# Loads by SyncE and casts by GpSimd for pairs 4 to 7, a preferred score bank, the last row tile in columns, and a new order of units, in an attention and MLP-mixer kernel

## The chip, the cores and the metric

The kernel runs on one core of a Trainium2 chip. Times are device microseconds of one execution; "before" is the median of three runs. A profile is one more execution, taken by the hardware profiler. Engines are named as the profile names them: PE (TensorE matmul) and PEld (its weight load), DVE (VectorE), ACT (ScalarE), POOL (GpSimd), SP (SyncE). A trailing q (SPq, POOLq) means the engine's sequencer, which issues DMAs.

## The reference

Attention over 4 batches of 8 heads, 768 positions and 64 features, with a window of 128 keys and 4 sink keys, then an MLP mixer on the result (512 features in all): token mixing through 256 hidden tokens and channel mixing through 1536 hidden channels.

```python
scores = scale * np.matmul(q, k.transpose(0, 1, 3, 2))
keep = is_sink | in_window              # pos < 4, or 0 <= query - key < 128
scores = np.where(keep, scores, -1000000000.0)
a = softmax(scores)
x = np.matmul(a, v)                     # heads side by side: (4, 768, 512)
...
h = np.maximum(xt @ w_tok1, 0.0) @ w_tok2
u = x + h.transpose(0, 2, 1)
h2 = np.maximum(u @ w_ch1, 0.0) @ w_ch2
return u + h2
```

## The kernel before

**The work and its units.** Two heads of one batch make a pair; there are 16 pairs (p), four to a batch. For each pair q and k are loaded in rows, made bf16, and turned so that features lie on partitions (qT, kT). Scores are taken in three groups (g = 0, 1, 2) of two key tiles each, masked, put through exp, and multiplied with v, which carries a column of ones for the sums. The mixer works on a batch: hidden tokens (tile h1T), u, u turned (tile uT), hidden channels (tile v1T), and the output rows, six tiles of 128.

**The order of TensorE** is written out by hand in ORDERED (L47 to L56), as numbered units of named streams:

- s, m, t, o: the first four pairs (batch 0): scores, masks added by matmul, q or k turned (12 matmuls of L530), values. o5 and o6 are pair 2's two halves of values, s12 is pair 3's last score group.
- g, h: batch 0's token mixing for the first and second half of the features. g2 to g4 and h2 to h4 make u; g5 to g7 and h5 to h7 turn it (four matmuls each, L146).
- a: pairs 4 to 15. a0 and a1 turn pair 4's q and k; a2 turns pair 5's q and k (24 matmuls, L548) and takes pair 4's first scores; a4 and a8 do so for the pairs after. From pair 8 on (BY_DMA, L61) q and k are turned by DMA transposes on SP (L476) instead.
- k: token mixing of the later batches. c: 24 units a batch of hidden channels (4 matmuls with w_ch1). x: 24 units a batch of output (3 matmuls of 512 columns with w_ch2, four units to a row tile).

Everything else (which engine evicts, when a DMA is issued, which PSUM bank is taken) is settled when the program is written, by a planner (class Plan, L275): it holds costs in ns for each operation, a model of the DMA queue with eight transfers under way at most (LANES, L251), and at each step commits the operation that can begin first. Its times are not measured; they only fix each engine's order. Each engine then runs its own list strictly in order.

**PSUM.** Two score tiles of two banks each (sc0, sc1; L80) and four further banks. `Plan.choose` (L300) takes for a score group the score tile that was free first; a late unit may take a bank of sc1. Groups g = 1 and 2 of pairs 4 and up are written in quarters (matmuls on 64 keys, four side by side) when they fall on sc0 and in halves (128 keys) otherwise (by_halves and by_quarters, L586 to L611).

**Loads.** Pairs 0 to 3: q and k come as fp32 through SP (load_raw, L111; eight transfers of 384 KB) and are cast by ACT, DVE or POOL (cast, L1218). Pairs 4 to 15: POOL issues DMAs that cast to bf16 on the way (load_cast, L125; two for each q and each k, 96 KB each as landed). v (L133) and the weights (w_tok1, w_tok2, four quarters of w_ch1, four of w_ch2) are casting DMAs of POOL too. A POOL DMA waits until the one issued eight before it has landed. The order in which POOL's loads are queued is written at L1222 to L1245: v of pairs 1 to 3 with the token weights between, then pair 4 and the first two w_ch1 quarters, pair 5 and the other two, pairs 6 and 7, w_ch2, and the remaining pairs.

**The end.** `whole` (L1139) computes an output row tile: 12 matmuls of 512 columns into one bank, an addition of u on DVE (L1152), a store by SP (L1158).

All matmuls go through `mm` and stand at L143 in the profile; copies and casts stand at L150 (ACT) and L152 (DVE, POOL).

Of the kernel before, what the change touches and what calls it, by code (L numbers as in the profile page):

```python
# [16 lines left out]
def kernel(  # L17
# [29 lines left out]
    ORDERED = (  # L47
# [8 lines left out]
    )  # L56
# [194 lines left out]
    LANES = 8  # L251
    TURN, STORE = 1300.0, 700.0
    CROWDED = 2.4
# [5 lines left out]
    class Op:  # L259
        def __init__(self, cost, fn, deps=(), then=(), size=0.0, lag=None, loads=0, traffic=0.0):  # L260
            self.cost, self.fn, self.deps, self.then = cost, fn, list(deps), list(then)
            self.done = None
            self.lag = SEM if lag is None else lag
            self.size = size
            self.urgent = 0
            self.loads, self.traffic = loads, traffic
            self.need = {}
            self.half = False

    def landed(at):  # L270
# [4 lines left out]
    class Plan:  # L275
# [128 lines left out]
    def burst(*pieces):  # L404
# [6 lines left out]
        def run():  # L411
# [5 lines left out]
            [t for p in pieces for t in p.then], half=True,  # L417
        )
        for p in pieces:
            for key in p.keys:  # L420
                done[key] = op
# [157 lines left out]
    def scores(p, g):  # L579
# [70 lines left out]
        deps += [done["mask", p, g]] if by_pe else []  # L650
        return piece((190, 165, 140)[g] if quarters else width(g) * 0.47, run, deps, {} if by_pe else {"sc": [[x]]}, then, [("s", p)])

# [149 lines left out]
    def mix_h(b, g, t0, n):  # L802
# [26 lines left out]
        done.setdefault(("h", b, g), []).append(op)  # L829
        return unit(n * NT * cn * 0.422, run, of_group(b, g) + [done["tok1"]], {"mx": [[op]]}, [op])  # L830


    def mix_u(b, g, s0, n, by_pe=False):
# [26 lines left out]
        if pairs[BY_DMA][0] <= b:  # L860
# [7 lines left out]
            for half in range(s0 // QH, (s0 + n - 1) // QH + 1):  # L868
                done.setdefault(("uT", b, half), []).append(then[-1])
        return unit(n * (NTOK + by_pe) * cn * 0.422, run, done["h", b, g] + [done["tok2"]], {"mx": [[op]]}, then)  # L870

# [109 lines left out]
    def mix_channels(b):  # L981
        units = []

        def v1(ft, half):
# [18 lines left out]
            done["v1", b, ft, half] = op  # L1003
            return unit(648, run, done["uT", b, half] + [done["ch1", ft * NW // NF]], {"mx": [[op]]}, [op])

# [52 lines left out]
        def products(t0, n):  # L1058
# [42 lines left out]
            def product(m, bank_name, op, before, stored=()):  # L1101
                a_name, b_name = TERMS[m]
                units = []
                for c in range(2):
# [20 lines left out]
                    if before is not None:  # L1125
                        deps.append(before)
                    units.append(unit(
                        n * KC * 110, run, deps, {"mx": [banks[bank_name]]} if before is None and c == 0 else {},
                        [op, *stored] if c else [],
# [9 lines left out]
        def whole(st):  # L1139
# [24 lines left out]
            for f0 in range(0, NF, KC):  # L1164
                deps = [done["v1", b, ft, h] for ft in range(f0, f0 + KC) for h in range(2)]
                deps.append(done["ch2", f0 // KC])
                parts.append(unit(
                    KC * 216, lambda f0=f0: run(f0), deps, {"mx": [[o]]} if f0 == 0 else {},
                    [o, sent] if f0 == NF - KC else [],
                ))  # L1170
            return parts

        for c in range(2):
# [27 lines left out]
    plan = Plan()  # L1201
    plan.free.update(PE=3000.0, ACT=2200.0, DVE=3900.0, POOL=4100.0)
    plan.queue = 12200.0
# [13 lines left out]

    def cast(p, n, at):  # L1218
        cost = {"POOL": 850.0} if p == NHP - 1 else {"DVE": 570.0} if p or n else {"ACT": 850.0}
        return Op(cost, lambda e: copy(e, bf_tile(p, n), raws[p][n]), [landed(at)])  # L1220

    for p, at in enumerate(((3900.0, 5300.0), (7500.0, 8600.0), (11300.0, 12500.0), (13500.0, 14700.0))):  # L1222
        for n, name in enumerate(("q_bf", "k_bf")):
            queue((name, p), cast(p, n, at[n]))
    v_sink = Op({"POOL": 650.0}, lambda e: copy(e, v_sink0, v_sink_f), [landed(9000.0)])
# [106 lines left out]
```

## Time and profile before

| what | value |
|---|---|
| median of three runs | 207.27 us (206.79 to 207.35) |
| profiled execution: its time, its span | 206.17 us, 204.4 us |
| granted TensorE clock | 0.997 |
| busy: PE, DVE, ACT, POOL | 194.3, 103.0, 104.7, 75.2 us |
| instructions: PE, DVE, ACT, POOL | 1925, 228, 182, 110 |
| moved by DMA | 26.27 MB, 92261 packets, 82512 of them under 512 B |

The span runs from the first to the last instruction; the execution's own time has some 1.8 us around it. Rows of a timeline give start, length, engine, line, operation, output<-input, shape and count, and in brackets the idle time of the engine just before and what ended it. "Idle" is told from modelled ends of matmuls, so short gaps inside a run of matmuls don't show as idle. The DMA share is the mean of the busy shares of 16 DMA engines; it goes over 1 because several transfers of one engine overlap.

### The profile page before, as it was taken

Reading aid. Unit: us, or ns where it says so; the run is one execution under the profiler, and the core shown is the slowest. Engines: PE = TensorE matmul, PEld = TensorE weight load, DVE = VectorE, ACT = ScalarE, POOL = GpSimd, SP = SyncE. Lnnn points to the kernel's source line nnn. Section 1 sums busy time; section 2 is a strip of 40 time slices with the busy share of each in tenths; the row PEclk is TensorE's granted clock in tenths of the full one; section 3 lists DMA queues with packets and bytes.
Section 4 is the critical chain, followed back from the end, with each engine's and each line's share of the span. In section 5 each row is a group of like instructions: output and inputs, shape, how many; then the busy total and the mean of one; then the engine's idle time right before and its main releaser. Section 6 shows DMA issues by size and latency. Waiting matters only on the chain.

```text
span 204.4 us, 4672 instructions
## 1 busy us (share of the span) xinstructions
PE 194.3 (95%) x1925; PEld 114.0 (56%) x1945; DVE 103.0 (50%) x228; ACT 104.7 (51%) x182; POOL 75.2 (37%) x110
## 2 busy tenths in 40 slices
PE   6889898999999999999999999999999999999992
PEld 1356585666665654656655654666665455565440
DVE  4877656685676655533477675625532433001221
ACT  4967767877866115777772442567632003673000
POOL 6299958795695564664612040000000000000000
PEclk9999999999999999999999999999999999999998
DMA  5999999999999999999995663201021622100222
GB/s 201 290 254 186 171 177 190 157 175 200 159 136 126 156 162 240 138 155 212 156 113 108 181 125 111 79 2 26 3 49 54 106 103 83 47 0 3 103 103 103
DMA packets 92261, 26.27 MB, mean 129 GB/s; under 512 B 82512, under 2 KB 89168, under 8 KB 92240
## 3 DMA queue, kind: packets, MB, share of 16 engines
q0 software_dynamic: 67232, 11.80, 74.1%
q1 hardware_dynamic: 25008, 14.17, 31.2%
q8 instruction: 15, 0.25, 0.5%
q14 instruction: 6, 0.05, 0.1%
HBM read 26.75 MB, written 6.29 MB: 162 GB/s over the span
## 4 chain that ended last, share of the span: by engine, by line
PE 85%; DMA 5%; POOL 4%; DVE 2%; issue 1%; ACT 1%; SPq 0%; POOLq 0%
PE ps_mx L143 74%; PE ps_sc L143 9%; DMA q_bf<-in_q_dram 3%; DMA v_sink_f<-in_v_dram 2%; POOL v_aug L136 2%; POOL w_tok L161 1%; DVE kT L152 1%; PE ps_mx L518 0%; PE ps_mx L548 0%; PE ps_mx L146 0%; SPq L222 0%; POOL k_bf L152 0%; POOL q_bf L152 0%; POOL q_bf L128 0%; DVE o_sb L1152 0%
## 5 line engine op out<-in xcount | busy, mean ns | idle before, releaser
L143 PE MATMUL ps_mx<-w_ch,v1T 128*128 128x512 bf16 x271 | 65.1, 379 | 1.1 <-issue 0.3
L143 PE MATMUL ps_mx<-uT,w_ch 128*128 128x384 bf16 x352 | 62.7, 326 | 0.6 <-DVE uT L152 0.6
L619 ACT ACTIVATE pT<-ps_sc 128x1024 bf16<-128x1024 f32 (+1 forms) x48 | 44.0, 952 | 26.5 <-PE ps_sc L143 26.3
L156 ACT ACTIVATE v1T<-ps_mx 128x384 bf16<-128x384 f32 x74 | 36.2, 492 | 36.3 <-PE ps_mx L143 36.0
L143 PEld LDWEIGHTS <-w_ch 128*128 128x128 bf16 x384 | 36.2, 98 | 24.3 <-issue 2.0
L143 PEld LDWEIGHTS <-v1T 128*128 128x128 bf16 x288 | 27.1, 98 | 28.9 <-issue 0.6
L1152 DVE TENSOR_TENSOR o_sb<-ps_mx,u_sb 128x512 f32<-128x512 f32 x24 | 16.6, 690 | 37.2 <-PE ps_mx L143 35.2
L128 POOL DMA_DIRECT2D k_bf<-in_k_dram x24 | 19.7, 828 | 11.1 <-DMA v_aug<-in_v_dram 7.7
L128 POOL DMA_DIRECT2D q_bf<-in_q_dram x24 | 19.8, 835 | 8.4 <-DMA k_bf<-in_k_dram 4.2
L143 PEld LDWEIGHTS <-w_tok 128*128 128x128 bf16 x192 | 18.4, 98 | 6.2 <-issue 0.9
L850 DVE TENSOR_TENSOR u_sb<-ps_mx,x_sb 128x512 bf16<-128x512 f32 x19 | 12.9, 687 | 16.0 <-PE ps_mx L143 16.0
L136 POOL DMA_DIRECT2D v_aug<-in_v_dram x16 | 16.8, 1053 | 3.0 <-PE ps_mx L143 2.8
L143 PE MATMUL ps_sc<-qT,kT 64*128 64x256 bf16 (+2 forms) x240 | 16.7, 258 | 0.3
L143 PEld LDWEIGHTS <-pT 128*128 128x128 bf16 x352 | 14.2, 98 | 3.7 <-DVE x_sb L704 0.7
L637 DVE TENSOR_TENSOR pT<-pT,mask_main 128x1024 bf16<-128x1024 bf16 (+1 forms) x24 | 14.2, 618 | 2.4 <-ACT pT L619 2.4
L143 PE MATMUL ps_mx<-v_aug,pT 128*128 128x65 bf16 x297 | 13.7, 194 | 0.9 <-DMA v_aug<-in_v_dram 0.9
L158 DVE TENSOR_SCALAR v1T<-ps_mx 128x384 bf16<-128x384 f32 x14 | 7.8, 556 | 12.4 <-PE ps_mx L143 12.2
L143 PE MATMUL ps_mx<-h1T,w_tok 128*128 128x256 bf16 x92 | 13.7, 272 | 0.0
L143 PEld LDWEIGHTS <-kT 64*128 64x128 bf16 (+1 forms) x240 | 6.1, 98 | 10.9 <-issue 8.8
L143 PE MATMUL ps_mx<-x_sb,w_tok 128*128 128x256 bf16 x96 | 12.0, 273 | 0.0
L744 DVE TENSOR_TENSOR x_sb<-ps_mx,recip 128x384 bf16<-128x384 f32 x17 | 9.4, 554 | 0.3
L152 POOL COPY kTs<-kT 64x4 bf16<-64x4 bf16 x10 | 3.2, 321 | 16.0 <-DMA kT<-k_bf 15.6
(76 smaller groups left out, 148.5 us busy)
## 6 DMA issues: line engine op xcount, KB each, us to landing
out_dram<-o_sb SPq DMA_DIRECT2D x24, 256.0 KB, 2.2
v_aug<-in_v_dram POOLq DMA_DIRECT2D x16, 192.0 KB, 8.5
w_ch<-in_moe_w_ch_dram POOLq DMA_DIRECT2D x8, 384.0 KB, 8.9
q_bf<-in_q_dram POOLq DMA_DIRECT2D x24, 96.0 KB, 9.3
k_bf<-in_k_dram POOLq DMA_DIRECT2D x24, 96.0 KB, 8.2
q_f<-in_q_dram SPq DMA_DIRECT2D x4, 384.0 KB, 5.4
k_f<-in_k_dram SPq DMA_DIRECT2D x4, 384.0 KB, 6.0
w_tok<-in_moe_w_tok_dram POOLq DMA_DIRECT2D x2, 384.0 KB, 7.1
```

The costliest lines, as they stand in the source:

```text
L128: in_order(nc.gpsimd.dma_start(out=out[:, h], in_=rows[:, h]))
L136: in_order(nc.gpsimd.dma_start(out=v_aug.rearrange("p i t d -> p (i t) d")[:, :, 0:D], in_=v[b].rearrange("h s d -> (h s) d")[2 * hp * S:2 ...
L143: in_order(nc.tensor.matmul(*args, skip_group_check=True, **kwargs))
L152: in_order({"DVE": nc.vector, "POOL": nc.gpsimd}[e].tensor_copy(out=out, in_=in_))
L156: in_order(nc.scalar.activation(out, in_, AF.Relu))
L158: in_order(nc.vector.tensor_scalar_max(out=out, in0=in_, scalar1=0.0))
L161: return in_order(nc.gpsimd.dma_start(out=out, in_=in_))
L619: in_order(nc.scalar.activation(part(tiles["pT", p][:, :, ds(2 * g, 2)]), of_keys(tiles["ps_s", p, g])[:, :, 0:width(g)], AF.Exp, scale=scale,
L637: in_order(nc.vector.tensor_tensor(out=pt, in0=pt, in1=m, op=ALU.mult))
L744: in_order(nc.vector.tensor_tensor(out=x_sb[b][:, :, ds((2 * hp + i) * D, D)], in0=tiles["ps_o", p, i][:, :, 0:D], in1=tiles["recip", p, i ...
L850: in_order(nc.vector.tensor_tensor(out=u_part(b, g, s0, n), in0=tiles["ps_u", b, g, s0], in1=x_sb[b][:, s0:s0 + n, c0:c0 + cn], op=ALU.add,))
L1152: in_order(nc.vector.tensor_tensor(out=o_sb.rearrange("p (g c) -> p g c", g=2), in1=u_rows(b, st), in0=tiles["ps_out", b, st].rearrange("p ...
```

## The change

1. q and k of pairs 4 to 7 are loaded by SP as fp32 into the two buffers that pair 3's q and k came in, and cast by POOL. Each load waits for the cast that empties its buffer: pair 4's k goes into the buffer of pair 3's q, pair 4's q into that of pair 3's k, and so on crosswise, so that at most two are under way. POOL's casting DMAs for these pairs go; only v stays there. Pair 8 and later are as before.
2. For pairs 0 to 3, the casts may go to DVE or POOL (the first to ACT). In the program that comes out, pair 1's q is cast by POOL instead of DVE and pair 3's q by DVE instead of POOL.
3. Of the score tiles that are free by the time TensorE gets there, the first is taken; the planner's costs tell groups on sc0 and sc1 apart.
4. The last row tile of the last batch is computed in three pieces of columns (256, 128, 128), each with its own bank, addition and store.
5. ORDERED is another order, and some of the planner's costs and landing times are other numbers. Units o5, s12 and o6, which followed a0, stand ahead of it now, and h6 and g7, which followed a2, ahead of a2.

What becomes of POOL's list up to pair 5's k, as the programs have it: before, v0, v1, v2, w_tok1, v3, cast of q3, w_tok2, cast of k3, then the DMAs of q4, k4, v4, two w_ch1 quarters, q5, k5, v5, two w_ch1 quarters; after, v0, cast of q1, v1, v2, w_tok1, v3, w_tok2, cast of k3, v4, two w_ch1 quarters, v5, cast of k4, two w_ch1 quarters, cast of q4, v6, v7, the first w_ch2 quarter, cast of q5, the second and third w_ch2 quarters, cast of k5.

```diff
     ORDERED = (
-        "t0-1 m0 s0 m1 s1 t2 m2 t3 s2 m3 o0 m4 s3 t4 o1 s4 o2 t5 m5-6 s5-6 o3 t6 m7 o4 m8 s7 t7 s8 g0 s9 g1 s10 "
-        "m9-10 s11 a0 o5 s12 o6-7 g2 o8 g3-5 h0-1 a1 g6 h2-5 a2 h6 c0 h7 c1 a3 c2-3 g7 c4-6 a4 c7-9 a5-6 c10-13 "
...
-        "x70-71 c75-83 x72 c84-95 x73-95"
+        "t0-1 m0-1 s0 t2 s1 t3 m2 s2 o0 m3 t4 s3 m4 s4 o1-2 m5 t5 s5 m6 s6 t6 m7 t7 s7 m8 o3 s8 o4 s9-10 m9 g0 "
+        "m10 o5 s11 o6 s12 g1 a0 o7-8 g2-4 h0-1 a1 g5 h2-3 g6 h4-6 g7 a2 c0 h7 c1-4 a3 c5-10 a4-5 c11 a6 c12-15 "
...
+        "k23 x66 c73 x67-69 c74 x70-71 c75-86 x72 c87-95 x73-94"
     )
...
-                            free.append((max(halves), n))
+                            free.append((max(*halves, self.free["PE"]), n))
...
+            wider = sum(w for w, n in zip(op.wider, given["sc"]) if n)
             op.fn()
-            self.free["PE"] = t + op.cost["PE"] + SWITCH * (op.half != self.half)
+            self.free["PE"] = t + op.cost["PE"] + wider + SWITCH * (op.half != self.half)
...
+        def columns(st, c0, cn):
+            g, o = c0 // C2, c0 % C2
+            def run():
+                tiles["ps_out", b, st, c0] = bank("mx", cn)
+                for ft in range(NF):
+                    mm(
+                        tiles["ps_out", b, st, c0], tiles["v1", b][:, ft, ts(st, P)], w_ch2[:, ft, c0:c0 + cn],
+                        start=(ft == 0), stop=(ft == NF - 1),
+                    )
+            def add(e):
+                o_sb = tiles["o_sb", b, st, c0] = osb_pool.tile([P, cn], FP32, name=f"o_sb{st}_{c0}")
+                in_order(nc.vector.tensor_tensor(
+                    out=o_sb, in1=u_rows(b, st)[:, g, o:o + cn], in0=tiles["ps_out", b, st, c0], op=ALU.add,
+                ))
+            def store(e):
+                in_order(nc.sync.dma_start(out=out[b, ds(st * P, P), c0:c0 + cn], in_=tiles["o_sb", b, st, c0]))
...
-            x = [u for st in range(NT) for u in whole(st)]
+            last = b == B - 1
+            x = [u for st in range(NT - last) for u in whole(st)]
+            if last:
+                x += [columns(NT - 1, c0, cn) for c0, cn in ((0, 2 * P), (2 * P, P), (3 * P, P))]
...
+    def load_later(p, n):
+        def load(e):
+            f = raws[p - 1][1 - n]
+            raws.setdefault(p, [None, None])[n] = f
+            in_order(nc.sync.dma_start(
+                out=f.rearrange("p h j d -> p h (j d)"), in_=rows_of(p, n).rearrange("p h j d -> p h (j d)"),
+            ))
+        return Op({"SP": 450.0}, load, [done[("k_bf", "q_bf")[n], p - 1]], traffic=LOAD)
...
+    for p in range(NHP, BY_DMA):
+        for n, name in enumerate(("q_bf", "k_bf")):
+            loaded = load_later(p, n)
+            plan.pending.append(loaded)
+            queue((name, p), cast(p, n, [loaded]))
...
     for n in range(2):
-        queue_pair(NHP + n)
+        queue(("v", NHP + n), load_values(NHP + n))
         for w in range(NW // 2 * n, NW // 2 * (n + 1)):
             queue(("ch1", w), load_weights(lambda w=w: load_ch1(w)))
     for n in range(2, NHP):
-        queue_pair(NHP + n)
+        queue(("v", NHP + n), load_values(NHP + n))
```

More of the change, by code (lines that the diff above doesn't have):

```diff
@@ L418, in burst @@
         )
+        op.wider = [w for p in pieces for w in p.wider]
         for p in pieces:
@@ L869, in mix_u @@
                 done.setdefault(("uT", b, half), []).append(then[-1])
-        return unit(n * (NTOK + by_pe) * cn * 0.422, run, done["h", b, g] + [done["tok2"]], {"mx": [[op]]}, then)
+        return unit(n * (NTOK + by_pe) * cn * 0.432, run, done["h", b, g] + [done["tok2"]], {"mx": [[op]]}, then)
     def turned_u(b, g):
@@ L1003, in v1 @@
             done["v1", b, ft, half] = op
-            return unit(648, run, done["uT", b, half] + [done["ch1", ft * NW // NF]], {"mx": [[op]]}, [op])
+            return unit(664, run, done["uT", b, half] + [done["ch1", ft * NW // NF]], {"mx": [[op]]}, [op])
         NH = NF // 2
@@ L1127, in product @@
                     units.append(unit(
-                        n * KC * 110, run, deps, {"mx": [banks[bank_name]]} if before is None and c == 0 else {},
+                        n * KC * 111, run, deps, {"mx": [banks[bank_name]]} if before is None and c == 0 else {},
                         [op, *stored] if c else [],
@@ L1171, in whole @@
             return parts
+        def columns(st, c0, cn):
[6 more added lines that the diff above has]
+                        start=(ft == 0), stop=(ft == NF - 1),
+                    )
+            def add(e):
[5 more added lines that the diff above has]
+                in_order(nc.sync.dma_start(out=out[b, ds(st * P, P), c0:c0 + cn], in_=tiles["o_sb", b, st, c0]))
+            added = Op({"DVE": 155.0 + 1.05 * cn}, add)
+            done["mixed", b, st] = added
+            deps = [done["v1", b, ft, h] for ft in range(NF) for h in range(2)]
+            deps += [done["ch2", w] for w in range(NW)]
+            return unit(
+                NF * (cn / 2.4 + 4.0), run, deps, {"mx": [[added]]},
+                [added, Op({"SP": 360.0}, store, [added], traffic=STORE * cn / DM)],
+            )
         for c in range(2):
@@ L1201 @@
     plan = Plan()
-    plan.free.update(PE=3000.0, ACT=2200.0, DVE=3900.0, POOL=4100.0)
+    plan.free.update(PE=3000.0, ACT=2200.0, DVE=3900.0, POOL=4700.0, SP=8300.0)
     plan.queue = 12200.0
```

25 lines of the change are left out of this document (16 added, 9 removed), and 10 rows, old and new, of the table ORDERED.

## The prediction

> **What bounds the kernel now.** I read the page first, then the busy times by stretch, TensorE's and GpSimd's timelines and the DMA rows.
>
> ```profile
> span 204.4 us, 4672 instructions
> PE 194.3 (95%) x1925; PEld 114.0 (56%) x1945; DVE 103.0 (50%) x228; ACT 104.7 (51%) x182; POOL 75.2 (37%) x110
> ...
> PE 85%; DMA 5%; POOL 4%; DVE 2%; issue 1%; ACT 1%; SPq 0%; POOLq 0%
> ```
>
> TensorE is busy for 95% of the span and holds 85% of the chain that ended last. What a new order can win is therefore TensorE's idle time and the tail, not its work. The stretches say where the idle time lies (columns: length, busy of each engine with instructions, granted clock, DMA share, GB/s):
>
> ```profile
> 5.00:10.00 5.00, 4.32 (x70) 1.98 (x71) 4.38 (x14) 4.48 (x8) 1.31 (x2) 1.00 1.35 287
> 10.00:15.00 5.00, 4.22 (x67) 2.52 (x66) 3.78 (x10) 3.57 (x7) 5.00 (x7) 1.00 1.73 265
> 15.00:20.00 5.00, 4.53 (x81) 2.98 (x81) 3.69 (x11) 3.53 (x6) 5.00 (x7) 1.00 1.68 187
> 20.00:25.00 5.00, 4.26 (x73) 2.75 (x73) 3.00 (x8) 4.12 (x6) 4.60 (x7) 1.00 2.17 166
> 25.00:30.00 5.00, 5.00 (x73) 4.34 (x69) 2.92 (x8) 2.56 (x5) 2.79 (x5) 1.00 1.73 183
> 30.00:35.00 5.00, 4.15 (x61) 2.96 (x58) 3.03 (x8) 3.79 (x10) 4.71 (x6) 1.00 1.76 186
> 40.00:200.00 160.00, 158.89 (x1460) 92.76 (x1471) 75.29 (x153) 76.13 (x133) 45.22 (x69) 1.00 0.93 110
> ```
>
> From 5 to 35 us TensorE is idle for 0.68 + 0.78 + 0.47 + 0.74 + 0 + 0.85 = 3.5 us; from 40 to 200 us for 1.1 us in all. So the opening is the place where this change can pay, and it is also where the DMA engines are full: the DMA share stays above 1 in each of the first six rows.
>
> ```profile
> 23.02 0.35 PE L530 MATMUL ps_mx<-ident,q_bf 64*128 64x64 bf16 x12 [0.69 <-DMA q_bf<-in_q_dram]
> 23.31 0.36 PE L143 MATMUL ps_mx<-v_aug,pT 128*128 128x65 bf16 x6
> ...
> 24.48 0.40 PE L143 MATMUL ps_mx<-v_aug,pT 128*128 128x65 bf16 x8
> ...
> 31.87 0.42 PE L548 MATMUL ps_mx<-ident,q_bf 64*128 64x64 bf16 x12
> ...
> 32.63 0.40 PE L146 MATMUL ps_mx<-ident,u_sb 128*128 128x128 bf16 x4
> ...
> 33.96 0.48 PE L143 MATMUL ps_mx<-uT,w_ch 128*128 128x384 bf16 x2 [0.61 <-DVE uT L152]
> 34.29 0.39 PE L146 MATMUL ps_mx<-ident,u_sb 128*128 128x128 bf16 x4
> 34.51 0.81 PE L143 MATMUL ps_mx<-uT,w_ch 128*128 128x384 bf16 x4
> ```
>
> On TensorE's timeline (start, length, in brackets the idle time before and what ended it) two waits stand out. The 0.69 us at 23.02 is unit a0 waiting for pair 4's q. Units o5, s12 and o6 follow it from 23.31 to about 24.6, where the row at 24.48 goes over into o7. At 31.87 unit a2 begins (pair 5's q and k turned, pair 4's first scores), at 32.63 h6, then c0, the first channel unit, with its 0.61 us for uT; h7 is at 34.29 and c1 at 34.51.
>
> **The change, part by part.**
>
> *Loads of pairs 4 to 7.* On GpSimd the old path looks like this:
>
> ```profile
> 14.92 0.84 POOL L152 CAST k_bf<-k_f 128x768 bf16<-128x768 f32 x1
> 15.68 1.67 POOL L128 DMA_DIRECT2D q_bf<-in_q_dram  x2
> 17.35 1.63 POOL L128 DMA_DIRECT2D k_bf<-in_k_dram  x2
> 18.97 1.03 POOL L136 DMA_DIRECT2D v_aug<-in_v_dram  x1
> 19.97 1.53 POOL L161 DMA_DIRECT2D w_ch<-in_moe_w_ch_dram  x2
> ...
> 27.66 0.75 POOL L161 DMA_DIRECT2D w_ch<-in_moe_w_ch_dram  x1 [0.73 <-DMA w_ch<-in_moe_w_ch_dram]
> ```
>
> Sixteen issues of about 0.82 us leave GpSimd (13.1 us) and eight casts of 0.84 us come (6.7 us), so it has 6.4 us less to do. GpSimd is not on the chain but for 4%, so this in itself is worth nothing; it matters through what it lets start earlier. SyncE gets eight issues of about 0.4 us; behind them in its queue stands nothing before pair 8's transposes, far later. What the transfers themselves cost is the question:
>
> ```profile
> 6.00:9.00 3.00, 2.81 (x48) 1.25 (x42) 2.52 (x9) 2.90 (x5) 0.31 (x1) 1.00 1.54 249
> 9.00:12.00 3.00, 2.47 (x28) 1.05 (x25) 1.78 (x6) 2.34 (x5) 3.00 (x4) 1.00 1.11 380
> 20.00:46.00 26.00, 24.41 (x329) 16.73 (x332) 17.46 (x40) 19.30 (x39) 21.32 (x27) 1.00 1.96 174
> ...
> w_ch<-in_moe_w_ch_dram POOLq DMA_DIRECT2D x8, 384.0 KB, 8.9
> ```
>
> From 9 to 12 us SyncE's fp32 loads have the engines nearly alone: 380 GB/s, so 384 KB (393,000 bytes) take 1.03 us. From 20 to 46 us GpSimd's casting loads run at 174 GB/s (counted in bf16), so the 192 KB of one q or k take 1.13 us. One load costs the same engine time either way, 0.1 us less at best. The transfers are not made cheaper; they are moved ahead of the weights. The Trainium skill (Trainium Kernel Development and Optimization, Key Constraints) states this against the change: DMAs from SyncE, ScalarE and GpSimd share the same 16 engines, and issuing from several only saves issue time. The two rates agree with it; by that rule alone the loads would bring nothing, and the sum would be the tail's term below.
>
> *Unit a0.* In the new order units o5, s12 and o6 stand ahead of a0. GpSimd casts pair 3's k right after its landing (14.4 us), and from there to the end of pair 4's q cast come 0.84 + 1.03 + 1.53 + 1.03 + 0.84 + 1.53 + 0.84 = 7.6 us: 22.0 us, if SyncE's loads are there, which can go out once pair 3's q and k are cast, about 14 and 15.3 us. TensorE reaches a0 later than that: 23.02 - 0.69, plus about 1.3 us for the three units. So the wait of 0.69 us goes.
>
> *Unit a2: what is late next.* a2 needs pair 5's k, cast by GpSimd at the end of v6, v7, the first ch2 quarter, q5's cast, and the second and third ch2 quarters (22.0 + 1.03 + 1.03 + 0.76 + 0.84 + 1.52 + 0.84 = 28.0 us if nothing waits). But in the old trace the 0.73 us before 27.66 is a GpSimd issue that waited for the landing of the transfer issued eight before it (the first of the two w_ch loads of the row at 19.97). By the same count the third ch2 quarter waits for the second w_ch1 load, which in the old run was issued near 20.7 and, at the median of 8.9 us, landed near 29.6. In the new order pair 4's q and k no longer stand ahead of it in that queue (two times 1.13 us, minus 2.3), but four SyncE loads use the same engines (4 x 1.03, plus 4.1), of which the last is partly behind it: about 31.0 us. Then 0.3 us until GpSimd goes on (the gap between such a landing and the issue; an estimate), 0.76 us for the issue and 0.84 us for the cast: k5 stands at 32.9. a2 turns q first (some 0.3 us), so it begins effectively at 32.6.
>
> TensorE would be there sooner: 31.87, less the 0.69 us, plus 0.44 us for the two transposing units h6 and g7 that the new order puts ahead of a2 (0.22 each, as from 34.29 to 34.51): 31.6, or earlier if more of the 3.5 us goes. So a wait of about 1 us stands at a2 in place of the one at a0. On the other hand all of uT is then ready, and the 0.61 us before 33.96 goes. Compared at the same work done (a2, h6, g7, c0, h7): the old run is there at 34.51 with g7 still to do, so 34.73; the new one at 32.6 + 0.76 (a2, as from 31.87 to 32.63) + 0.65 (c0, four matmuls of 0.163: the last row's four take 0.33 us longer than the two at 33.96) + 0.22 (h7) = 34.23. **Opening: -0.5 us**, with ends at +1.7 (rival B) and -2.5 (rival A at its best).
>
> *Score banks.* Of the 24 later score groups (pairs 4 to 15, g = 1 and 2), 12 were written in quarters before (7 of g = 1, 5 of g = 2) and 12 are now (all of g = 1); the program's matmuls show it. The array's column time of a group falls from 512 to 384 columns in g = 1 and from 384 to 288 in g = 2, at 0.163 us for 384 (c0, above) 54 and 41 ns. Five groups swap, 5 x 13 ns: 0.07 us, so nothing.
>
> *Tail.*
>
> ```profile
> 200.77 0.69 DVE L1152 TENSOR_TENSOR o_sb<-ps_mx,u_sb 128x512 f32<-128x512 f32 x1 [1.90 <-PE ps_mx L143]
> ...
> L744 DVE TENSOR_TENSOR x_sb<-ps_mx,recip 128x384 bf16<-128x384 f32 x17 | 9.4, 554 | 0.3
> ...
> out_dram<-o_sb SPq DMA_DIRECT2D x24, 256.0 KB, 2.2
> ```
>
> A matmul of 512 columns takes 0.217 us by c0's 0.163 for 384, 12 of them 2.6 us. In columns they are 12 of 256 (half of that) and 24 of 128 (0.056: four in the 0.22 us of h7): 1.3 + 1.35 = 2.65, at most +0.1 us. The last addition shrinks from 512 to 128 columns. From 0.69 us at 512 and 0.554 at 384 the slope is 1.06 ns a column, so 0.28 us: -0.4 us. The last store is 64 KB instead of 256; at the 380 GB/s above that is 0.17 instead of 0.69 us, of which I count 0.4 because the trace shows no store this small. **Tail: -0.7 us**, ends -0.9 and -0.3.
>
> *The rest of the order, the cost constants, casts moved between engines.* From 40 to 200 us TensorE has 1.1 us of idle time that any order could win, and new waits could add as much. The casts of pair 1's q (to GpSimd) and pair 3's q (to VectorE) change engines in a stretch where VectorE is busy 3.7 to 4.4 of 5 us; this is inside the opening's ends. I take 0, ends -0.6 and +0.6.
>
> **Sum:** -0.5 - 0.7 + 0 = -1.2 us. The profiled execution took 206.17 us around its span of 204.4, so 205.0 on that run; it lies 1.1 us under the median of the three timed runs, 207.27, and against that median the forecast is **206.1 us**.
>
> **Rivals.**
> *A, k5 is in time.* The weights land as early as before, so nothing is waited for at a2. For it: GpSimd has 6.4 us less to issue. Against it: the DMA share of 1.7 to 2.2. Opening -1.5 (the 1 us more) to -2.5, with the tail about -2.4: 204.9, down to 204.1.
> *B, the SyncE loads push the weights back (slower).* Mixed traffic may cost more than each alone: the row from 6 to 9 us, with both kinds under way, shows 249 GB/s; a load at that rate takes 1.58 us, four of them 2.2 us more. The second w_ch1 load lands at 33.2, a2 begins 2.2 us later, and +1.7 - 0.7 gives 208.3. It decides from a landing of about 32.2 on (-0.5 becomes +0.7); beyond that each us costs a us. The Trainium skill (DMA: Bandwidth & Descriptors, Queues, rings and completion order) says that each engine goes round between its queues packet by packet, which would hold GpSimd's queue to part of its rate for as long as SyncE's loads last. That is this rival's mechanism; the row from 6 to 9 us has both kinds side by side but doesn't show who yields.
> *C, only the tail.* The opening's gain is eaten at a2 or later, as TensorE had no idle time to lose after 40 us. -0.7 to -0.3: about 206.8.
>
> **How the numbers follow.** A measurement here tells about 0.3% (0.62 us) from no change: faster is under 206.65, slower over 207.89. Forecast (205.4 to 206.65) 0.40, A 0.16, C 0.20, B 0.24. Faster: 0.40 + 0.16 + 0.03 of C = 0.59. Same: 0.17 of C and 0.03 of B = 0.20. Slower: 0.21. The range, 204.3 to 208.4, takes in A but for its best end and B up to its price; under 0.2 is left out.
>
> **What would show it.** In the new profile: no wait of L533 (old L530) for q at about 23 us; a wait of about 1 us at a2 for GpSimd's k_bf, and ahead of it GpSimd idle before a w_ch issue for a w_ch landing; no wait for uT in c0; idle time from 5 to 35 us about 3 us; the last addition about 0.28 us. If a2 doesn't wait, A; if it waits over 2 us, B. The forecast is wrong if TensorE gains idle time after 40 us.

## The result, and the profile after

The changed kernel takes **209.37 us** (median; 208.95 to 209.37) where the kernel before took 207.19 us beside it (206.79 to 207.35): a ratio of **1.0101, 95% interval 1.0078 to 1.0125**. It is slower by about 2.1 us, and the time lies above the range given (204.3 to 208.4). (A fourth execution fell in a slower state of the chip, 212.2 us at a granted clock of 0.991, and isn't counted.) The profiled execution took 209.36 us around a span of 207.7, so 3.2 us more than the profiled one of before; one us of that is because that one lay 1.1 us under its own median.

The same lines of the page as before:

```profile
span 207.7 us, 4734 instructions
PE 193.8 (93%) x1949; PEld 114.7 (55%) x1969; DVE 102.6 (49%) x227; ACT 105.7 (51%) x190; POOL 67.7 (33%) x100
...
PE 79%; DMA 11%; DVE 3%; ACT 2%; issue 1%; POOL 1%; SPq 1%; POOLq 0%; ACTq 0%
PE ps_mx L143 67%; PE ps_sc L143 10%; DMA q_f<-in_k_dram 4%; DMA kT<-k_bf 4%; DMA k_f<-in_k_dram 3%; SPq L115 1%; ACT pT L622 1%; DVE kT L152 1%; PE ps_mx L551 1%; PE ps_mx L533 1%; DVE k_bf L152 0%; DVE qT L152 0%; PE ps_mx L521 0%; ACT qT L150 0%; DVE q_bf L152 0%
```

TensorE does the same work (193.8 us busy after 194.3); what has grown is the share of DMA on the chain, 5% to 11%, and the line names three of them: `q_f<-in_k_dram` (a k loaded into a q buffer, which only the new loads do), `kT<-k_bf` (the transposed k of a later pair) and `k_f`. The busy times by stretch say how much time that is (columns as before):

```profile
5.00:10.00 5.00, 3.13 (x62) 1.45 (x62) 3.06 (x10) 2.60 (x6) 1.43 (x3) 1.00 1.27 263
10.00:15.00 5.00, 4.32 (x70) 2.16 (x72) 3.99 (x9) 4.81 (x7) 5.00 (x7) 1.00 1.59 283
15.00:20.00 5.00, 4.78 (x92) 2.81 (x90) 4.63 (x15) 4.51 (x8) 4.21 (x5) 1.00 1.68 196
20.00:25.00 5.00, 3.77 (x49) 2.60 (x48) 2.74 (x7) 3.28 (x5) 1.35 (x2) 1.00 1.51 234
25.00:30.00 5.00, 3.20 (x57) 2.95 (x58) 1.88 (x5) 1.58 (x3) 4.44 (x6) 1.00 1.38 227
30.00:35.00 5.00, 4.65 (x61) 3.86 (x59) 2.66 (x6) 3.42 (x10) 3.57 (x5) 1.00 1.46 230
40.00:200.00 160.00, 157.23 (x1460) 91.68 (x1478) 75.94 (x155) 79.24 (x143) 42.80 (x65) 1.00 0.89 111
```

From 5 to 35 us TensorE is now idle for 30 - 23.85 = 6.15 us (before 3.52), and from 40 to 200 us for 2.8 us (before 1.1). So 2.6 us more idle time come from the opening and 1.7 from one later place. The list of TensorE's waits (engine, line and what released it; us in total, times, longest) names two waits for the opening and one for the later place, and its timeline shows where they stand:

```profile
PE ps_mx L533 <- POOL q_bf L152: 4.2, 2, 3.0
PE ps_mx L143 <- DVE pT L640: 1.7, 1, 1.7
```

```profile
8.55 0.35 PE L533 MATMUL ps_mx<-ident,q_bf 64*128 64x64 bf16 x12 [1.25 <-POOL q_bf L152]
...
26.80 0.35 PE L533 MATMUL ps_mx<-ident,q_bf 64*128 64x64 bf16 x12 [2.98 <-POOL q_bf L152]
...
35.78 0.82 PE L143 MATMUL ps_mx<-uT,w_ch 128*128 128x384 bf16 x4
36.44 0.39 PE L146 MATMUL ps_mx<-ident,u_sb 128*128 128x128 bf16 x4
36.66 0.65 PE L143 MATMUL ps_sc<-uT,w_ch 128*128 128x384 bf16 x3
...
64.56 0.29 PE L143 MATMUL ps_mx<-v_aug,pT 128*128 128x65 bf16 x4 [1.66 <-DVE pT L640]
```

**At t2** (8.55) TensorE waits 1.25 us for pair 1's q, which GpSimd now casts; this is the 1.2 us that the first row is short of (3.13 busy, before 4.32). Version 2 below, with the old loads, has 0.87 us of this wait too, so the new loads don't make it; the rows from 10 to 20 us and from 30 to 35 us win about 0.85 us back.

**At a0** TensorE waits 2.98 us for pair 4's q, where it waited 0.69 before and where the prediction had no wait at all. The 0.61 us for uT ahead of c0 (now at 35.78, no bracket) are gone, as forecast. GpSimd's timeline, and SyncE's queue beside it, show what a0 waited for:

```profile
14.88 0.84 POOL L152 CAST k_bf<-k_f 128x768 bf16<-128x768 f32 x1
...
23.65 0.83 POOL L152 CAST k_bf<-q_f 128x768 bf16<-128x768 f32 x1 [4.44 <-DMA q_f<-in_k_dram]
24.41 1.50 POOL L161 DMA_DIRECT2D w_ch<-in_moe_w_ch_dram  x2
25.89 0.85 POOL L152 CAST q_bf<-k_f 128x768 bf16<-128x768 f32 x1
```

```profile
14.59 0.37 SPq L1270 DMA_DIRECT2D q_f<-in_k_dram  x1
15.75 0.37 SPq L1270 DMA_DIRECT2D k_f<-in_q_dram  x1
24.50 0.37 SPq L1270 DMA_DIRECT2D q_f<-in_q_dram  x1
```

SyncE issues k4 and q4 (k and q of pair 4) at 14.59 and 15.75, about as the prediction had it (14 and 15.3). But GpSimd then stands idle for 4.44 us until k4 has landed, 9 us after its issue; k4's cast, two w_ch1 issues and q4's cast follow one behind another, and q4's cast ends at 26.74 instead of 22.0. The 4.44 us are nearly all of that difference. And the next load goes out only after k4's cast, at 24.50, because the new loads reuse the two raw buffers of the pair before them: each pair pays a landing and a cast in turn. The packets of the two queues in this stretch (q0 is GpSimd's, q1 SyncE's; packets, MB, share of the 16 engines), first from 14.5 to 18.3 us, then from 18.5 to 22.5:

```profile
q0 software_dynamic: 2728, 0.62, 183.5%
```

```profile
q0 software_dynamic: 1045, 0.39, 80.3%
q1 hardware_dynamic: 456, 0.67, 53.4%
```

For 3.7 us after the first issue SyncE's loads have not moved a packet; then both loads move together at 0.67 MB in 4 us, 168 GB/s, less than half of the 380 GB/s that the prediction took from the stretch where they had the engines alone. GpSimd's queue falls meanwhile from 163 GB/s (0.62 MB in 3.8 us) to 98: the median time from a w_ch issue to its landing rises from 8.9 to 15.8 us.

**At a14** the wait of 1.66 us is for a mask that VectorE does late. Its timeline:

```profile
63.39 0.53 DVE L152 COPY kTs<-kT 64x4 bf16<-64x4 bf16 x2 [3.27 <-DMA kT<-k_bf]
63.95 0.56 DVE L640 TENSOR_TENSOR pT<-pT,mask_main 128x768 bf16<-128x768 bf16 x1
```

VectorE stands 3.27 us in a small copy of sink columns until a DMA transpose lands, with the mask queued behind it. The planner may give this copy to GpSimd or VectorE, by its model of when each is free; the new loads and costs changed that model.

**The tail**: the last addition is down from 0.69 to 0.29 us.

```profile
203.85 0.29 DVE L1194 TENSOR_TENSOR o_sb<-ps_mx,u_sb 128x128 f32<-128x128 f32 x1 [0.25 <-PE ps_mx L143]
204.52 0.29 DVE L1194 TENSOR_TENSOR o_sb<-ps_mx,u_sb 128x128 f32<-128x128 f32 x1 [0.38 <-PE ps_mx L143]
```

From its end (204.81) to the end of the span are 2.9 us, and before, from 201.46 to 204.4, also 2.9. The smaller store is faster all the same. From the list of DMA issues (number, size, median us from issue to landing; 2.2 us for 256 KB):

```profile
out_dram<-o_sb SPq DMA_DIRECT2D x2, 64.0 KB, 1.6
```

The last one lands 1.56 us after its issue (204.84 to 206.40); the last one of 256 KB took 2.0 us (201.49 to 203.51, where SyncE's wait for it ends). But in the trace SyncE has six more semaphore waits behind that one now, which stood ahead of it before, and they take the 0.4 us again.

### The profile page after: what moved, and what is told of

Same layout as the page of the kernel before. It is cut to its first block, busy times and chain, and to the rows that moved or that the text cites. A ratio compares the mean times of both kernels' runs of the same rounds, so it can differ in the third digit from the quotient of the medians.

```text
span 207.7 us, 4734 instructions
## 1 busy us (share of the span) xinstructions
PE 193.8 (93%) x1949; PEld 114.7 (55%) x1969; DVE 102.6 (49%) x227; ACT 105.7 (51%) x190; POOL 67.7 (33%) x100
## 4 chain that ended last, share of the span: by engine, by line
PE 79%; DMA 11%; DVE 3%; ACT 2%; issue 1%; POOL 1%; SPq 1%; POOLq 0%; ACTq 0%
PE ps_mx L143 67%; PE ps_sc L143 10%; DMA q_f<-in_k_dram 4%; DMA kT<-k_bf 4%; DMA k_f<-in_k_dram 3%; SPq L115 1%; ACT pT L622 1%; DVE kT L152 1%; PE ps_mx L551 1%; PE ps_mx L533 1%; DVE k_bf L152 0%; DVE qT L152 0%; PE ps_mx L521 0%; ACT qT L150 0%; DVE q_bf L152 0%
## 5 line engine op out<-in xcount | busy, mean ns | idle before, releaser
L143 PE MATMUL ps_mx<-w_ch,v1T 128*128 128x512 bf16 (+2 forms) x283 | 63.5, 361 | 1.1 <-issue 0.3
L143 PEld LDWEIGHTS <-v1T 128*128 128x128 bf16 x312 | 28.5, 98 | 27.3 <-issue 0.8
L1159 DVE TENSOR_TENSOR o_sb<-ps_mx,u_sb 128x512 f32<-128x512 f32 x22 | 15.1, 687 | 33.1 <-PE ps_mx L143 33.1
L143 PEld LDWEIGHTS <-w_tok 128*128 128x128 bf16 x192 | 18.3, 98 | 6.0 <-issue 1.0
L143 PE MATMUL ps_sc<-qT,kT 64*128 64x256 bf16 (+1 forms) x240 | 16.7, 259 | 0.1
L640 DVE TENSOR_TENSOR pT<-pT,mask_main 128x768 bf16<-128x768 bf16 (+1 forms) x23 | 14.2, 651 | 2.4 <-ACT pT L622 2.4
L128 POOL DMA_DIRECT2D k_bf<-in_k_dram x16 | 13.3, 841 | 3.4 <-DMA v_aug<-in_v_dram 2.3
L143 PE MATMUL ps_mx<-v_aug,pT 128*128 128x65 bf16 x264 | 12.5, 194 | 1.7 <-DVE pT L640 1.7
L128 POOL DMA_DIRECT2D q_bf<-in_q_dram x16 | 13.3, 845 | 0.2 <-issue 0.2
L640 DVE TENSOR_TENSOR pT<-pT,mask_first 128x1024 bf16<-128x1024 bf16 x13 | 9.3, 717 | 3.6 <-ACT pT L622 3.5
L143 PE MATMUL ps_mx<-x_sb,w_tok 128*128 128x256 bf16 x84 | 10.5, 273 | 0.1
## 6 DMA issues: line engine op xcount, KB each, us to landing
w_ch<-in_moe_w_ch_dram POOLq DMA_DIRECT2D x8, 384.0 KB, 15.8
```

Source lines behind the costliest of these rows:

```text
L128: in_order(nc.gpsimd.dma_start(out=out[:, h], in_=rows[:, h]))
L143: in_order(nc.tensor.matmul(*args, skip_group_check=True, **kwargs))
L640: in_order(nc.vector.tensor_tensor(out=pt, in0=pt, in1=m, op=ALU.mult))
L1159: in_order(nc.vector.tensor_tensor(out=o_sb.rearrange("p (g c) -> p g c", g=2), in1=u_rows(b, st), in0=tiles["ps_out", b, st].rearrange("p ...
```

## The experiments

Times are medians with the ratio to the kernel before, timed beside them, and its interval. Theory L: SyncE's loads land late. Rival O: the new order itself costs the time. Rival S (the prediction's B): what SyncE's loads win, GpSimd's lose.

**1. The tail alone.** The kernel before with `columns` for the last row tile.

```diff
-            x = [u for st in range(NT) for u in whole(st)]
+            last = b == B - 1
+            x = [u for st in range(NT - last) for u in whole(st)]
+            if last:
+                x += [columns(NT - 1, c0, cn) for c0, cn in ((0, 2 * P), (2 * P, P), (3 * P, P))]
```

> The kernel before with one edit, the last row tile in columns; loads, order and casts are as before. The prediction's tail term (-0.4 for the addition, -0.4 for the smaller store, +0.1 for TensorE) gives 207.2 - 0.7 = 206.5 us. Rival: only the addition counts, because from the end of the last addition to the end of the span the traces of before and after both show 2.9 us: 207.2 - 0.4 + 0.1 = 206.9 us.

Measured: 207.11 us, 0.9995 (0.9971 to 1.0018). The interval just leaves out the 206.5 of the prediction's tail term and holds the rival's 206.9: the tail is worth 0.1 us, at most 0.6.

**2. The old loads in the new order.**

```diff
-    for p in range(NHP, BY_DMA):
-        for n, name in enumerate(("q_bf", "k_bf")):
-            loaded = load_later(p, n)
-            plan.pending.append(loaded)
-            queue((name, p), cast(p, n, [loaded]))
...
-        queue(("v", NHP + n), load_values(NHP + n))
+        queue_pair(NHP + n)
```

> The changed kernel, but q and k of pairs 4 to 7 are loaded with a cast by GpSimd as in the kernel before; the unit order, the tail and the cost constants stay those of the change. Theory L (late loads: SyncE's fp32 loads land 7 to 9 us after their issue while GpSimd's queue is full, and a0 waits 3.0 us): that wait falls under 1 us, 209.4 - 2.2 = 207.2 us or less. Theory O (the new order itself costs the time): within 0.5 us of 209.4. If the wait of 1.7 us before a14 goes too (VectorE's copy of kTs may fall elsewhere), 205.5 us.

Measured: **206.11 us, 0.9945 (0.9932 to 0.9958)**. TensorE's timeline at a0 and the two stretches:

```profile
23.90 0.35 PE L533 MATMUL ps_mx<-ident,q_bf 64*128 64x64 bf16 x12
```

```profile
5.00:35.00 30.00, 26.59 (x416) 17.67 (x416) 20.54 (x52) 21.85 (x40) 22.84 (x27) 1.00 1.73 213
40.00:200.00 160.00, 158.51 (x1470) 92.71 (x1486) 75.05 (x151) 77.01 (x140) 44.75 (x72) 1.00 0.95 110
```

a0 doesn't wait: GpSimd's load of q4, issued at 15.0, lands at 23.7 and needs no cast. The wait at a14 is gone too, since here the copy of kTs comes elsewhere in VectorE's order. Rival O falls: everything but the loads (order, tail, score banks, casts of pairs 0 to 3, constants) makes the kernel 1.1 us faster, of which the tail is 0.1, and with the new loads it loses 3.3 us.

**3. The new loads in the old order.** `ORDERED` of the kernel before (its last unit taken off), all else as in the change.

> The changed kernel with the unit order of the kernel before (less one unit at the end); loads by SyncE, casts and tail are those of the change. Theory L: pair 4's q still stands at about 26.7 us and TensorE reaches a0 at about 22.3, so a0 waits 3.5 to 4.5 us and the time is 209.4 or more, up to 211. Theory O: the time falls to the kernel before less the tail, 206.8 us.

Measured: 215.49 us, 1.0380 (1.0342 to 1.0418). O falls again, but my numbers missed: this is 4 us over the upper end, and a0 waits 1.71 us instead of 3.5 to 4.5. TensorE's row at a0 and the three us from 27 on show a second price, a granted clock of 0.51 after that wait:

```profile
25.38 0.35 PE L533 MATMUL ps_mx<-ident,q_bf 64*128 64x64 bf16 x12 [1.71 <-POOL q_bf L152]
```

```profile
27.00:30.00 3.00, 3.00 (x37) 2.58 (x34) 1.68 (x5) 0.93 (x2) 1.74 (x3) 0.51 1.23 259
```

VectorE shows the larger one:

```profile
64.39 0.60 DVE L152 COPY kTs<-kT 64x4 bf16<-64x4 bf16 x2 [3.80 <-DMA kT<-k_bf]
```

The wait for the transposed k is there as well, three times and 8.0 us in all on VectorE, and TensorE is idle for 5.6 us from 40 to 200 us (before 1.1). The planner has put ten of these copies on VectorE here; before it was six. That this is the whole of the 8 us isn't shown.

**4. The copy of kTs on GpSimd.**

```diff
-                {"POOL": 300.0, "DVE": 300.0}, sinks_of, done["kT", p] + [("sk", p - NHP)],
+                {"POOL": 300.0}, sinks_of, done["kT", p] + [("sk", p - NHP)],
```

> The changed kernel, but the copy kTs of pairs 8 to 15 may go to GpSimd only, not to VectorE. If the 1.66 us before a14 come from VectorE standing in that copy until the transposed k lands, ahead of the mask that a14 needs, they go: 209.4 - 1.7 = 207.7 us, and a0's 3.0 us stay. Rival: another wait takes their place (the mask's own inputs, or k still landing), 209.2 us or more.

Measured: 207.41 us, 1.0018 (0.9990 to 1.0046), so 1.7 us less by the ratios (1.0101 to 1.0018). In its trace a14 doesn't wait, and the idle time from 40 to 200 us is back at 1.1 us:

```profile
5.00:35.00 30.00, 24.82 (x404) 16.42 (x403) 19.05 (x49) 20.97 (x37) 20.10 (x24) 1.00 1.49 242
40.00:200.00 160.00, 158.90 (x1471) 92.88 (x1486) 75.52 (x149) 77.77 (x141) 44.92 (x70) 1.00 0.91 112
```

The opening keeps 5.2 us of idle time, against 3.4 with the old loads: a0 waited 1.05 us in this execution, with k4 landing at 22.0 instead of 23.65. The remaining 1.5 us (1.0018 to 0.9945) are the loads' own price. It is not a sharp figure: the four of version 4's ten executions with a granted clock of 0.999 or 1.00 took 206.7 to 207.1 us, 0.8 us above version 2, and the six at 0.992 took 206.8 to 209.3. What lowered their clock no kept trace shows.

**5 and 6. All eight loads early.** Each takes the raw buffer of the pair four before it, free long since; 6 has the edit of 4 as well.

```diff
-            f = raws[p - 1][1 - n]
+            f = raws[p - NHP][n]
...
-        return Op({"SP": 450.0}, load, [done[("k_bf", "q_bf")[n], p - 1]], traffic=LOAD)
+        return Op({"SP": 450.0}, load, [done[("q_bf", "k_bf")[n], p - NHP]], traffic=LOAD)
```

> The changed kernel, but each fp32 load of pairs 4 to 7 takes the raw buffer of the pair four before it (free since that pair's cast) instead of the one that pair p-1's cast has just left; so SyncE can issue all eight loads by about 15 us instead of 14.6 to 43 us. Theory L (the loads are late by their own latency, one round trip of load and cast after the other): k4 and q4 stand before TensorE needs them, a0 waits under 1 us, 209.4 - 2.2 = 207.2 us or less, the 1.7 us before a14 stay if VectorE's copy of kTs still stands ahead of the mask. Theory S (the loads share the DMA engines with GpSimd's queue, so what they win the v, w_tok and w_ch loads lose, eight times 1 us or more): new waits for v_aug, w_tok or w_ch between 15 and 35 us, and 209.4 us or more.

> Both edits: the raw buffers of four pairs before, and kTs of pairs 8 to 15 on GpSimd only. By theory L both waits are gone: 205.5 to 206.2 us, level with the version with the old loads (206.1) or better. By theory S 207.4 us (the version with kTs on GpSimd alone) or more.

Measured: 215.94 us, 1.0419 (1.0391 to 1.0446), and 213.37 us, 1.0284 (1.0254 to 1.0315). The loads are out by 17.3 us and a0 waits for nothing, but rival S decides. In 5, TensorE's waits, the packets from 15 to 22 us, and two stretches:

```profile
PE ps_mx L143 <- DMA v_aug<-in_v_dram: 6.1, 1, 6.1
```

```profile
q1 hardware_dynamic: 1337, 1.93, 89.5%
q0 software_dynamic: 1392, 0.18, 38.5%
```

```profile
20.00:25.00 5.00, 0.62 (x11) 0.62 (x11) 0.00 (x0) 0.00 (x0) 2.38 (x4) 0.50 1.54 263
25.00:30.00 5.00, 4.78 (x40) 2.71 (x39) 2.20 (x5) 2.32 (x3) 2.95 (x4) 0.50 1.70 189
```

The engines took nearly as many packets from one queue as from the other, 1337 and 1392. But SyncE's are 1.4 KB each (1.93 MB by 1337) and those of a v load 0.13 KB, so GpSimd's queue got 26 GB/s beside SyncE's 276. Pair 1's v, issued at 10.0 us, landed at 24.3 and TensorE stood for 6.1 us. Its granted clock was 0.50 from 20 us on, within that wait, up to 30 us: the wait costs once more in slow work. So loads issued earlier are no way out here.

**7. The casts on VectorE** (`{"DVE": 570.0}` for the casts of pairs 4 to 7), so that GpSimd never waits for a landing.

> The changed kernel, but the casts of pairs 4 to 7 are VectorE's (0.56 us each) instead of GpSimd's (0.84), so that GpSimd never waits for a landing of SyncE's and issues its loads on. If GpSimd standing idle before its casts (4.4 us before k4's) is what costs the time, through the weights behind them: 207.5 us or less. If the landing of the fp32 loads itself is what TensorE waits for: a0 still waits 2 us or more, VectorE stands idle in place of GpSimd with the normalizations behind it, and the time is 209 to 211 us.

Measured: 213.15 us, 1.0266 (1.0234 to 1.0297), worse than I gave it. VectorE's cast of k4, TensorE's wait, and the two us after it:

```profile
22.70 0.56 DVE L152 CAST k_bf<-q_f 128x768 bf16<-128x768 f32 x1 [3.75 <-DMA q_f<-in_k_dram]
```

```profile
23.78 1.49 PE L143 MATMUL ps_mx<-x_sb,w_tok 128*128 128x256 bf16 x6 [3.18 <-DVE x_sb L711]
```

```profile
24.00:26.00 2.00, 2.00 (x14) 1.25 (x13) 1.48 (x3) 0.38 (x1) 1.32 (x2) 0.50 1.65 189
```

VectorE stands 3.75 us for k4 with the normalizations (x_sb) behind it, TensorE waits 3.18 us for those, and its clock is 0.50 after that. a0 itself, later now, doesn't wait. It is the landing that is late, and whichever engine waits for it in order holds up its own queue.

**8. The weights held back.** w_tok2, w_ch1 and w_ch2 are issued only after q4's cast.

```diff
+    for key in ["tok2", *(("ch1", w) for w in range(NW)), *(("ch2", w) for w in range(NW))]:
+        done[key].deps.append(done["q_bf", NHP])
```

> The changed kernel, but the loads of w_tok2, w_ch1 and w_ch2 are issued only after pair 4's q cast, so that GpSimd's queue holds only v and w_tok1 loads when SyncE issues k4 and q4 at 14.4 to 15.8 us. The time is not the point (weights come later, 209 us or more). If the 4 us between issue and first data, and the half rate after it, come from GpSimd's full queue, k4 and q4 land within 3 to 5 us of their issue (both by about 20 us) and their casts end by 21.5. If the latency is SyncE's own, q4's cast ends at 25 us or later as before.

Measured (one execution): 212.82 us, with TensorE waiting for w_tok. What counts are GpSimd's casts:

```profile
21.11 1.22 POOL L152 CAST k_bf<-q_f 128x768 bf16<-128x768 f32 x1 [5.77 <-DMA q_f<-in_k_dram]
22.51 0.83 POOL L152 CAST q_bf<-k_f 128x768 bf16<-128x768 f32 x1 [0.18 <-DMA k_f<-in_q_dram]
...
25.75 0.85 POOL L152 CAST q_bf<-q_f 128x768 bf16<-128x768 f32 x1
```

q4's cast ends at 23.3: between what the two theories said, since the v and w_tok1 loads were still in GpSimd's queue. The clean case is q5: issued at 22.36, when that queue was all but empty, it moved its first packet by 23.4 and was cast from 25.75 on, 3.4 us after its issue. In the changed kernel the same load went out at 24.50 and its cast began at 30.97, 6.5 us later. So about 3 us of the latency come with GpSimd's traffic.

**9 and 10. Half of the loads.** 9: SyncE loads only pairs 6 and 7, held by a small write of GpSimd to their raw buffers until the w_ch1 issues are out; 10: only pairs 4 and 5. The other two pairs are loaded with a cast as before.

```diff
-    for p in range(NHP, BY_DMA):
+    for p in range(NHP + 2, BY_DMA):
...
+    mark = Op(
+        {"POOL": 100.0},
+        lambda e: [in_order(nc.gpsimd.memset(raws[NHP - 1][n][0:1, 0:1, 0:1, 0:1], 0.0)) for n in range(2)],
+        [("ch1", NW - 1)],
+    )
```

```diff
-    for p in range(NHP, BY_DMA):
+    for p in range(NHP, NHP + 2):
```

> The changed kernel, but only pairs 6 and 7 are loaded as fp32 by SyncE, after the last w_ch1 issue (a small GpSimd write to their raw buffers holds them until then); pairs 4 and 5 are loaded by GpSimd as before. If the price of SyncE's loads lies in the opening, where pairs 4 and 5 are awaited, the time is that of the old loads in the new order, 206.1 to 206.6 us. If each such load costs wherever it stands (GpSimd stands before its casts, and its queue gets fewer bytes), half of the 3.3 us between the old and the new loads stays: 207.5 us or more.

> The other half: pairs 4 and 5 by SyncE, pairs 6 and 7 by GpSimd as before. If the price lies in the opening, a0 still waits 1.5 to 3 us: 207.4 to 209.4 us, 207.4 if VectorE's copy of kTs no longer stands ahead of the mask of a14 (here GpSimd makes that copy). If the two halves share the price, 207 or less.

Measured: 9: 215.56 us, 1.0377 (1.0332 to 1.0423); 10: 208.1 us, 1.0030 (0.9993 to 1.0067). 9 told nothing of the kind: my hold let the loads out only at 36.3 us, when TensorE was about to need them, and it waited 2.7 and 2.3 us for their casts. 10 is level with version 4 (1.0018), which has all eight loads; in both GpSimd makes the copy of kTs that held up a14. In version 10's kept trace, of an execution of 210.98 us, a0 waits 3.48 us. So pairs 4 and 5, in the opening, carry the price, and 6 and 7 no part that the intervals (0.6 to 0.8 us to each side) can show.

**11. Pair 1's q cast on VectorE**, on top of 2.

> The old loads in the new order (206.1 us) with pair 1's q cast on VectorE (0.57 us) instead of GpSimd (0.82), its k on GpSimd instead. The wait of 0.9 us before t2 should shrink by 0.25; if nothing later takes it up, 205.9 us. If k comes later by as much, 206.1 or a little more.

Measured: 206.97 us, 0.9981 (0.9944 to 1.0017), executions from 205.5 to 208.3: no gain on 2 that can be seen.

**12. Small pieces.** Version 5 with SyncE's loads in pieces of 256 bytes (raw rows padded from D to D + 1 floats), each load issued in two halves.

> The version with all eight SyncE loads early, with these loads cut into pieces of 256 bytes instead of 1536 (the raw rows are padded). There, from 15 to 23 us, GpSimd's v loads (pieces of 128 bytes) moved 25 KB per us and SyncE's 280, at nearly equal counts of pieces (192 and 191 in the us from 17). If the engines alternate piece by piece, the counts stay equal and the bytes become 1 to 2: v1 lands before 20 us instead of 24.3, and SyncE's loads take much longer (40 to 80 KB per us while both run). If the engines share by bytes or favour SyncE, v1 stays at 24 us or later.

Measured (one execution): 224.11 us. The packets from 15 to 22 us, and from 19 to 22 us:

```profile
q0 software_dynamic: 3386, 0.70, 113.4%
q1 hardware_dynamic: 1879, 0.47, 50.9%
```

```profile
q0 software_dynamic: 1126, 0.23, 85.7%
q1 hardware_dynamic: 1067, 0.27, 67.7%
```

Pair 1's v landed at 18.4 us instead of 24.3, and GpSimd's queue moved 0.70 MB instead of 0.18. Over the whole stretch the counts weren't equal (1.8 to 1), but SyncE's queue was thin at 16 to 18 us: an issue of half a load took 0.8 to 2.7 us instead of 0.4. From 19 to 22 us the counts are nearly equal, and so are the bytes, with pieces of 0.20 and 0.25 KB on average. That the size of the pieces decides who gets the bytes agrees with both runs; how much of v's earlier landing is due to SyncE's slower issues, this run can't separate.

**13. What a0 waits for.** Version 4 with the third and fourth w_ch1 issues after q4's cast.

```diff
+    for w in range(NW // 2, NW):
+        done["ch1", w].deps.append(done["q_bf", NHP])
```

> The version with kTs on GpSimd (207.4 us), with one more edit: the third and fourth w_ch1 issues, which stood on GpSimd between the casts of pair 4's k and q (two times 0.75 us), come after q's cast. In the changed kernel k4 had landed at 23.65 us, no later than the old path's q4 (23.7), and q4's cast ended 3.1 us later: k's cast, two issues, q's cast. Theory Q (this chain behind the landing, not the landing, is what a0 waits for): a0's wait shrinks by 1.5 us, to nothing from 1.05 and to about 1.5 from 3.0, and the time falls to 206.1 to 206.7 us. Theory L (the landing is what counts, and w_ch1 then comes too late or the wait moves to another cast): 207.2 us or more.

Measured: 207.2 us, 0.9979 (0.9946 to 1.0013), by the ratio 0.8 us less than 4, with overlapping intervals. The trace shows:

```profile
22.36 0.83 POOL L152 CAST k_bf<-q_f 128x768 bf16<-128x768 f32 x1 [3.17 <-DMA q_f<-in_k_dram]
25.30 0.83 POOL L152 CAST q_bf<-k_f 128x768 bf16<-128x768 f32 x1 [2.11 <-DMA k_f<-in_q_dram]
```

With the issues out of the way GpSimd waits 2.11 us for q4 itself, up to 25.30, and a0 still waits 2.37 us. In this execution q4 lands at about 25.25 us, some 1.5 us after the old path's, and then needs 0.83 us of cast: that is the 2.4 us. So Q's full gain isn't there. But Q doesn't fall either. A load of SyncE's signals its landing in 16 updates of a semaphore, and the trace has their times. For q4 the last came at 25.14 in the changed kernel and at 23.16 in version 4, and the casts began only at 25.89 and 24.21, behind the two issues: there the issues did cost 0.75 of a0's 2.98 us, and all of its 1.05. What varies between executions is the last signal: the first came at 21.44 to 21.70 in all three, the last at 23.16 to 25.25. The times, with overlapping intervals, can't tell how much Q is worth.

## Why the prediction was wrong

- **Unit a0: wrong, and the step that failed.** "22.0 us, if SyncE's loads are there": GpSimd's own chain was right, but the condition was never priced. I gave each load 1.03 us at 380 GB/s, a rate taken where the loads ran nearly alone; beside GpSimd's full queue they showed 3.7 us without a packet, then 168 GB/s for the two together, 9 us from issue to landing. So q4 stood at 26.74. The page of before had 5.4 us (q) and 6.0 us (k) from issue to landing for such loads, and I used neither; they would have put q4 near 23.8 us, an estimate (14.6 + 6.0 + 0.84 + 1.53 + 0.84), still too early. By the prediction's own measure (a2, h6, g7, c0 and h7 done) the opening is +1.9 us instead of -0.5: 36.66 us, where h7 ends now, against 34.73. The Trainium skill (DMA: Bandwidth & Descriptors, Queues, rings and completion order) had the point that I held against rival B only: an engine goes round between its queues by packets. Experiment 5 agrees (1337 packets to 1392, but 1.93 MB to 0.18), and 12 from 19 to 22 us (1067 to 1126); in the changed kernel the counts from 18.5 to 22.5 us were 456 to 1045, so packet for packet isn't the whole rule.
- **Unit a2: passed over.** a2 began at 35.00, behind a0's delay, with no wait of a us for k5. The stall that I looked for, GpSimd at a w_ch issue waiting for a landing, was taken up by longer waits at its casts.
- **The loads cost the engines the same: not tested, and of no use.** What a0 waited for was not 1.03 or 1.13 us of engine time, but a load's 9 us beside another queue.
- **Score banks: nothing.** No run isolates them, so this is neither confirmed nor refuted.
- **Tail: -0.7 was too much.** The addition gave its -0.4 (0.69 to 0.29). TensorE's +0.1 was right: the two last additions start 0.67 us apart, 12 matmuls of 128 columns at 0.056. The store's -0.4 is there at its landing (2.0 to 1.56 us) and lost again behind it, at SyncE's waits at the end. Experiment 1 measured 0.1 us in all.
- **The rest of the order: 0 +- 0.6 was wrong twice over.** Idle time after 40 us was the prediction's own sign of being wrong, and it came: 2.8 us after 1.1. The copy of kTs behind a DMA transpose costs 1.7 us (experiment 4, and the idle time from 40 to 200 us), which I could have looked for: the changed order of VectorE's instructions stands in the program and can be read before any run. Without it and without the loads the rest gives 1.0 us (experiment 2, less the tail).
- **The sum:** -1.0 for the order, -0.1 for the tail, +1.5 for the loads, +1.7 for the copy make +2.1. These are steps from one version's ratio to the next, each good to 0.3 to 0.6 us, so they add up by construction and prove nothing by it. The two profiles are a check: +1.9 at h7, +1.7 at a14 and -0.4 for the addition make the 3.2 us between them. Where the order's 1.0 us lies can't be shown: the profiled execution of before was 1.1 us faster than its median.
- **Rivals.** B had the right sign and cause but the wrong place: I priced what the weights lose (2.2 us, at a2), and SyncE's loads lost first. Neither B nor the forecast had a case in which both things go wrong, a0 and a late wait, so the range ended 1 us too low.

The best version is the new order with the old loads, 206.11 us, 0.55% under the kernel before.

## What to carry over

A load moved to another queue isn't free because the issuing engine is free: take its latency from a stretch in which the other queue is as full as it will be, and count the bytes of each piece, since here the queue with small pieces lost against the one with large ones. Put nothing that waits for a DMA landing ahead of urgent work on an engine that runs in order, be it a cast or a copy of eight columns; and where a planner assigns engines, compare each engine's order of instructions before and after, since a change of its costs moves more than the change says. When a change has several parts, build the versions with one part undone: here the order was a gain, hidden under the loads.

## What the runs showed of the hardware

- A queue of large pieces (1.4 KB on average) starved one of small pieces (0.13 KB): 276 GB/s against 26 while both had work (experiment 5).
- An fp32 load of 384 KB moved its first packet 3.7 us after its issue beside a busy GpSimd queue, and was being cast 3.4 us after its issue when that queue was empty (experiment 8). What the engines do in those 3.7 us stays open. Its landing is that of its last part: of k4's 16 signals in the changed kernel the first came at 20.29 and the last at 23.59.
- After a wait of 6.1 us TensorE's granted clock was 0.50 for the next 5 us (experiment 5); after one of 2.98 us, in the changed kernel, it stayed at 1.00. The Trainium skill (TensorE: Matmul & The Clock Gate, The HAM clock gate) gives a window of about 3.4 us of idleness for this. These two rows agree, but others don't: the clock was 0.50 for 2 us after a wait of 3.18 us (experiment 7) and 0.51 from 27 to 30 us after one of 1.71 us that ended at 25.4 (experiment 3). So a wait can cost more than its length, and its length alone doesn't tell whether it will.
